# First-layer products in PSUM tiles of their own, the work between products placed piece by piece, twelve plain steps

## The chip, the core and the metric

One core of a Trainium2 chip. Five engines work in parallel, each through its own instructions in order: PE (TensorE, matmuls into PSUM), DVE (VectorE), ACT (ScalarE), POOL (GpSimd) and SP (SyncE, which issues most DMAs). They wait for each other by semaphores. PSUM has eight banks of 128 x 512 f32. The metric is the time of one execution on the device in microseconds (us), the median of several runs.

## The reference

The input x is 2048 x 576 (S x D), f32.

```python
def layernorm(x): return (x - mean(x)) / sqrt(var(x) + 1e-5)      # over D
X = rfft2(layernorm(x)) * (w_r + 1j * w_i)
h = x + irfft2(X)
out = h + relu(layernorm(h) @ w1) @ w2      # w1 576 x 4608, w2 4608 x 576
```

## The kernel before, in words

**First part.** Normalisation, the forward Fourier transform along D and S as matmuls with constant matrices, the product with the filter, and the inverse transform. Its last rows are normalised again and transposed into four chunks `xc[0..3]` of 512 tokens; each chunk holds a high and a low part, since f32 products are made of three matmuls with fp32r operands: high x high, high x low, low x high. `split` (L321) makes such a pair: ACT copies with rounding (the high part), another engine subtracts (the low part, L323).

**The MLP in blocks.** The 4608 hidden units are 18 blocks `g` of 256. *Plain steps*, one per block and chunk, are listed in `steps` (L522): `mm1` (28 matmuls of 512 columns) makes the hidden values, `relu_split` (L560) splits them, `mm2` (48 matmuls of 288 columns) multiplies by w2, and DVE adds the result to `xs` in SBUF (L556). There are eight such steps, (0, 0) to (1, 2). During them `sum_jobs` prepares sums of chunks, stores them to DRAM and `load_sum` (L615) brings them back when wanted.

**Doubles.** From block `FIRST` = 2 on, two chunks are taken together (a *double*: block g, pair p) in 2 x 2 block form with seven products in place of eight, in both layers. `l1_prod(d, r)` (L727) is product r = 0..6 of the first layer of double d, six or eight matmuls of 512 columns, into one of the banks `a` (alternating between doubles), `b`, `c`:

- r = 0, 1, 3, 6 write `a`, each on top of the last: 0 makes A11 B11; once it is copied out (`p1`, L738), 1 adds S2 T2; once that is copied out (`u2`), 3 adds S3 T3; once that is copied out (`c2`), 6 adds A22 T4.
- r = 2 writes `c` (S1 T1); it is added to `c2` after r = 3 (L747); then r = 5 adds S4 B22 to `c`, which is added to `u2` (L756).
- r = 4 writes `b`; it is added to `p1` (L751).

The hidden values are relu of `p1`, `c2`, `u2` and of the final `a` ("late": only finished after r = 6). The second layer takes them, and sums of them, again in split form, for two hidden sets: Z (from `u2` and `c2`: A2, A11, and the sums S12, S34 that four POOL subtractions make in `hsum`, L731 to L734) and Y (from `p1` and the late `a`). `prod` (L789) is one second-layer product, six matmuls of 288 columns, into one of two PSUM tiles `wps[0]`, `wps[1]` in turn, on top of what stands there; `add` (L794) is the DVE addition into `xs`, which must be done before the next product goes into the same tile.

**The order.** It is the order of the Python code, per engine; nothing is rescheduled. `slot(d)` does for r = 0..6: first-layer product r of double d + 1, second-layer products 2r and 2r + 1 of double d with their adds, then `l1_late(d, r)` and `l1_post(d + 1, r)` (the copies, relus, sums and splits), then `weights(d, r)` (splits and sums for the next block: L644 to L648 and `w1_split` for w1, L677 to L680 and `w2_split` for w2; a block lasts two slots, even and odd, `turn` 0 and 1). So products 0 to 6 of the second layer belong to Z, 7 to 13 to Y, and Y's late part is split in the slot in which it is used. `slot_last` ends it with plain second-layer products. The last plain step, step 7, does the first layer of double 0 beside its own four `mm2`.

PSUM: one pool `ps` of four buffers of two banks each. `wps[2]` holds both `a` banks, `wps[3]` holds `b` and `c`. Waits follow tiles: an instruction that writes one half of such a tile also waits for readers of the other half.

Of the kernel before, what the change touches and what calls it, by code (L numbers as in the profile page):

```python
# [128 lines left out]
def kernel(ctx: ExitStack, tc: tile.TileContext, x, w_r, w_i, w1, w2, cc2, c1, fb, ib, c3, out):  # L129
    nc = tc.nc  # L130
    pool = ctx.enter_context(tc.tile_pool(name="sb", bufs=1))
    psum = ctx.enter_context(tc.tile_pool(name="ps", bufs=1, space=PSUM))
# [19 lines left out]
    def act(o, i, **kw):  # L152
        nc.scalar.activation(o, i, AF.Copy, **kw)  # L153
# [368 lines left out]
    steps = [(0, 0), (0, 1), (0, 2), (1, 1), (1, 0), (0, 3), (1, 3), (1, 2)]  # L522
    FIRST = 2
# [94 lines left out]
    wps = [None] * 4  # L618
# [87 lines left out]
    doubles = [(g, p) for g in range(FIRST, NG) for p in ((0, 1) if g % 2 == 0 else (1, 0))]  # L706
# [22 lines left out]
    def hsum(p0, p1, o):  # L729
        s1, s2, s3, s4 = (sums[:, 256 * k:256 * k + 256] for k in range(4))  # L730
        nc.gpsimd.tensor_add(s1, p0[:, 256:], p1[:, 256:])  # L731
        nc.gpsimd.tensor_sub(s2, s1, p0[:, :256])  # L732
        nc.gpsimd.tensor_sub(s3, p0[:, :256], p0[:, 256:])
        nc.gpsimd.tensor_sub(s4, p1[:, :256], s2)  # L734

    def l1_post(d, r):

        a, b, c = (l1_bank(d, n_) for n_ in "abc")  # L738
        p1, u2, c2 = fx["p1"][d % 2], fx["u2"], fx["c2"]
        Z, Y = HF["Z"], HF.get("Y")  # L740
        if r == 0:
            act(p1, a)
        elif r == 1:
            act(u2, a)
        elif r == 3:
            act(c2, a)
            nc.vector.tensor_add(c2, c2, c)  # L747
            relu(c2, c2)
            split(*Z["A2"], c2)
        elif r == 4:  # L750
            nc.vector.tensor_add(p1, p1, b)  # L751
            relu(p1, p1)
            if 0 < d < LAST:
                split(*Y["A11"], p1[:, :256])
        elif r == 5:
            nc.vector.tensor_add(u2, u2, c)  # L756
            relu(u2, u2)
            hsum(u2, c2, None)
            split(*Z["A11"], u2[:, :256])
        elif r == 6:  # L760
            split(*Z["S12"], sums[:, :512])
            split(*Z["S34"], sums[:, 512:])
            if d == LAST:
                split(*Y["S12"], p1)

    def l1_late(d, r):

        a = l1_bank(d, "a")
        p1, c2 = fx["p1"][d % 2], fx["c2"]
        Y = HF["Y"]  # L770
        if r == 0:
            relu_split(Y["A2"], a)
            if d < LAST:
                relu(c2, a)
                hsum(p1, c2, None)
        elif d < LAST:
            if r == 1:
                split(*Y["S12"], sums[:, :512])
            elif r == 2:
                split(*Y["S34"], sums[:, 512:])  # L780

    def prod(z, a, b, bank, first, end=True, whole=True):
        ah, al = a if isinstance(a, tuple) else HF[z][a]
        bh, bl = b if isinstance(b, tuple) else W2[b]
        P = wps[bank].rearrange("p (a n) -> p a n", a=2)[:, :, :288]
        for tt in range(2):
            q = slice(128 * tt, 128 * tt + 128)
            for n_, (l, r) in enumerate(((ah, bh), (ah, bl), (al, bh))):
                nc.tensor.matmul(P[:, tt], l[:, q], r, start=first and n_ == 0, stop=end and n_ == 2, skip_group_check=whole and not first)  # L789

    def add(c, bank, hs, hd):
        P = wps[bank].rearrange("p (a n) -> p a n", a=2)[:, :, :288]
        xt = xs[:, CH * c + 2 * hs:CH * c + 2 * hs + 2, 288 * hd:288 * hd + 288]
        nc.vector.tensor_add(xt, xt, P)  # L794

# [23 lines left out]
    def weights(d, r):  # L819

        g, p = doubles[d]
        if g == NG - 1:
            return
        turn = d % 2
        if turn:
            if r == 0 and g + 2 < NG:
                load_w1(g + 2, vs[1])
            if r == 2:
                w2_sums()
            if r == 4:  # L830
# [98 lines left out]
    for i in range(3, len(steps)):  # L929
        if i == 3:  # L930
            load_weights(FIRST)
            vs[1], vs[2] = raw[FIRST]
        if i == 5:
            vs["s"] = ebuf([128, 1152])
            w2_bufs()
            w2_sums()
        if i == 6:
            w1_bufs()
            w2_split("B22", nc.gpsimd)
            w2_split("T12", nc.gpsimd)  # L940
        if i < 7:
            for q in range(4):
                if q < 2:
                    mm1(i + 1, q)
                mm2(i, q)
                for _ in range(2 if i < 6 else 3):
                    if jobs:
                        jobs.pop(0)()
            continue
        while jobs:  # L950
            jobs.pop(0)()
        w2_split("T34", nc.gpsimd)
        w1_sums()
        for n_ in ("A11", "S12", "S34", "A2", "W4", "wd"):
            w1_split(n_, nc.gpsimd)
        load_w1(FIRST + 1, vs[1])
        FT = sb([128, 4096], "F", dt=F32R)
        TF.update(T1=khalf(3, 0), T2=khalf(1, 0))
        for k, n_ in ((0, "T3"), (1, "T4")):
            TF[n_] = tuple(v2d(FT[:, 2048 * k + 1024 * j:2048 * k + 1024 * j + 1024]) for j in range(2))  # L960
        for n_ in ("T2", "T1", "T3", "T4"):
            load_sum(doubles[0][1], n_)
        fbin = [ebuf([128, 1024]) for _ in range(2)]
        fx.update(p1=(fbin[0][:, :512], fbin[1][:, :512]), u2=fbin[0][:, 512:], c2=fbin[1][:, 512:])
        wps[2:] = [ps(), ps()]
        hidden_bufs("Z")
        for r in range(7):
# [3 lines left out]
            l1_post(0, r)  # L971
# [34 lines left out]
```

## Time and profile before

| | us |
|---|---|
| runs (3) | 1360.06 to 1363.88, median 1361.53 |
| profiled execution | 1363.99 |
| its span, first to last instruction | 1362.2 |
| mean granted PE clock | 0.914 |
| PE busy | 1071.8 (79%) |
| DVE busy | 808.0 (59%) |
| POOL busy | 548.4 (40%) |
| ACT busy | 452.2 (33%) |

In the chain of waits and the timeline a row is: start in us from the span's start, length in us, then engine, line and, in the timeline, operation, written tile <- read tiles, shape and count; in brackets the idle time of the engine before it and what ended that. Matmul lengths overlap, since they are pipelined: the pitch from one start to the next is what they cost when PE is full. The granted clock is a share of full speed. Tiles: `A` holds `xs` and the sums, `d` any PSUM tile, `X`, `B`, `C`, `F` chunks, their sums and second-layer weights, `D` hidden parts, `e` shared buffers (among them `p1`, `u2`, `c2` and the first-layer weights).

### The profile page before, as it was taken

Reading aid. Unit: us, or ns where it says so; the run is one execution under the profiler, and the core shown is the slowest. Engines: PE = TensorE matmul, PEld = TensorE weight load, DVE = VectorE, ACT = ScalarE, POOL = GpSimd, SP = SyncE. Lnnn points to the kernel's source line nnn. Section 1 sums busy time; section 2 is a strip of 40 time slices with the busy share of each in tenths; the row PEclk is TensorE's granted clock in tenths of the full one; section 3 lists DMA queues with packets and bytes.
Section 4 is the critical chain, followed back from the end, with each engine's and each line's share of the span. In section 5 each row is a group of like instructions: output and inputs, shape, how many; then the busy total and the mean of one; then the engine's idle time right before and its main releaser. Section 6 shows DMA issues by size and latency. Waiting matters only on the chain.

```text
span 1362.2 us, 17410 instructions
## 1 busy us (share of the span) xinstructions
PE 1071.8 (79%) x6702; PEld 926.5 (68%) x6702; DVE 808.0 (59%) x1181; ACT 452.2 (33%) x836; POOL 548.4 (40%) x658
## 2 busy tenths in 40 slices
PE   7999999567777777777777777777777777777777
PEld 6776889456666666666666666666666666666666
DVE  7688658525555555555555555555555565555555
ACT  5444442213232333333333333333333333333331
POOL 5005533514343445353435353534444444444421
PEclk8999999789999999999989999988888988888989
DMA  9824113370404040404041313131313222222224
GB/s 247 197 76 103 38 37 124 127 281 4 154 11 152 10 152 20 141 20 141 20 141 29 133 34 127 35 127 52 109 54 107 65 96 79 82 80 81 66 85 113
DMA packets 53987, 127.68 MB, mean 94 GB/s; under 512 B 5392, under 2 KB 25232, under 8 KB 53904
## 3 DMA queue, kind: packets, MB, share of 16 engines
q1 hardware_dynamic: 53168, 125.68, 29.4%
q8 instruction: 53, 0.87, 0.3%
q10 hardware_dynamic: 736, 0.89, 0.2%
q14 instruction: 30, 0.25, 0.1%
HBM read 113.43 MB, written 13.11 MB: 93 GB/s over the span
## 4 chain that ended last, share of the span: by engine, by line
PE 44%; DVE 21%; POOL 7%; ACT 6%; issue 4%; DMA 0%; DVEq 0%; SPq 0%; POOLq 0%
PE d L727 24%; PE d L789 19%; DVE A L794 10%; DVE X L323 5%; ACT e L566 3%; POOL A L732 2%; POOL A L731 2%; POOL A L734 2%; ACT X L153 2%; DVE D L563 1%; DVE e L751 1%; DVE e L747 1%; DVE e L756 1%; ACT e L153 1%; DMA B<-t0T 0%
## 5 line engine op out<-in xcount | busy, mean ns | idle before, releaser
L794 DVE TENSOR_TENSOR A<-A,d 128x576 f32<-128x576 f32 x445 | 332.1, 752 | 331.1 <-PE d L789 319.9
L727 PE MATMUL d<-B,e 128*128 128x512 f32 x528 | 189.5, 498 | 222.5 <-ACT e L153 163.1
L727 PEld LDWEIGHTS d<-B,e 128*128 128x128 f32 x528 | 118.4, 238 | 262.1 <-ACT e L153 170.5
L789 PE MATMUL d<-X,D 128*128 128x288 f32 x1548 | 264.8, 319 | 3.6 <-DVE D L563 2.0
L789 PEld LDWEIGHTS d<-X,D 128*128 128x128 f32 x1548 | 254.9, 214 | 18.0 <-DVE D L563 2.2
L153 ACT ACTIVATE e<-d 128x512 f32<-128x512 f32 (+2 forms) x144 | 85.0, 590 | 290.4 <-PE d L727 245.0
L323 POOL TENSOR_TENSOR X<-e,X 128x576 fp32r<-128x576 f32 (+1 forms) x49 | 74.4, 1532 | 239.1 <-ACT X L153 239.1
L566 ACT ACTIVATE e<-e 128x512 f32<-128x512 f32 x96 | 60.7, 632 | 312.1 <-DVE e L756 123.9
L731 POOL TENSOR_TENSOR A<-e,e 128x256 f32<-128x256 f32 x48 | 35.4, 737 | 264.8 <-ACT e L566 264.8
L323 POOL TENSOR_TENSOR e<-e,e 128x256 fp32r<-128x256 f32 (+2 forms) x65 | 86.7, 1344 | 123.6 <-ACT e L153 123.6
L727 PE MATMUL d<-F,e 128*128 128x512 f32 x384 | 99.4, 394 | 0.0
L727 PE MATMUL d<-X,e 128*128 128x512 f32 x304 | 81.0, 403 | 23.1 <-DVE e L751 23.1
L789 PEld LDWEIGHTS d<-X 128*128 128x128 f32 x576 | 83.1, 188 | 6.0 <-issue 0.8
L789 PE MATMUL d<-X 128*128 128x288 f32 x576 | 86.7, 295 | 0.6 <-DVE A L794 0.6
L789 PE MATMUL d<-X,e 128*128 128x288 f32 x496 | 84.7, 295 | 0.0
L727 PEld LDWEIGHTS d<-X,e 128*128 128x128 f32 x304 | 56.1, 195 | 36.1 <-DVE e L751 26.9
L727 PE MATMUL d<-C,e 128*128 128x512 f32 x224 | 61.1, 400 | 23.1 <-DVE e L747 23.1
L727 PEld LDWEIGHTS d<-F,e 128*128 128x128 f32 x384 | 68.8, 188 | 11.3
L789 PEld LDWEIGHTS d<-X,e 128*128 128x128 f32 x496 | 74.0, 188 | 2.7
L323 DVE TENSOR_TENSOR D<-A,D 128x512 fp32r<-128x512 f32 x63 | 66.8, 1060 | 1.3 <-ACT D L153 1.3
L323 DVE TENSOR_TENSOR X<-e,X 128x256 fp32r<-128x256 f32 (+2 forms) x48 | 41.5, 864 | 37.1 <-ACT X L153 36.7
L727 PEld LDWEIGHTS d<-C,e 128*128 128x128 f32 x224 | 39.9, 188 | 33.9 <-DVE e L747 26.8
(141 smaller groups left out, 1693.6 us busy)
## 6 DMA issues: line engine op xcount, KB each, us to landing
F<-t0T SPq DMA_DIRECT2D x36, 512.0 KB, 4.6
F<-t1T SPq DMA_DIRECT2D x32, 512.0 KB, 4.6
e<-in_B_w_dram SPq DMA_DIRECT2D x18, 576.0 KB, 3.8
e<-in_B_w_dram SPq DMA_DIRECT2D x18, 512.0 KB, 3.7
B<-t0T SPq DMA_DIRECT2D x18, 512.0 KB, 4.6
X<-t0T SPq DMA_DIRECT2D x18, 512.0 KB, 4.8
B<-t1T SPq DMA_DIRECT2D x16, 512.0 KB, 4.5
X<-t1T SPq DMA_DIRECT2D x16, 512.0 KB, 4.8
```

The costliest lines, as they stand in the source:

```text
L153: nc.scalar.activation(o, i, AF.Copy, **kw)
L323: eng.tensor_sub(l, v, h)
L563: nc.vector.scalar_tensor_tensor(l, p, 0.0, h, op0=ALU.max, op1=ALU.subtract)
L566: nc.scalar.activation(o, i, AF.Relu)
L727: nc.tensor.matmul(o, a, b, start=bool(first) and n_ == 0, stop=n_ == len(ops) - 1, skip_group_check=not first)
L731: nc.gpsimd.tensor_add(s1, p0[:, 256:], p1[:, 256:])
L732: nc.gpsimd.tensor_sub(s2, s1, p0[:, :256])
L734: nc.gpsimd.tensor_sub(s4, p1[:, :256], s2)
L747: nc.vector.tensor_add(c2, c2, c)
L751: nc.vector.tensor_add(p1, p1, b)
L789: nc.tensor.matmul(P[:, tt], l[:, q], r, start=first and n_ == 0, stop=end and n_ == 2, skip_group_check=whole and not first)
L794: nc.vector.tensor_add(xt, xt, P)
```

## The change

Five things, all in the MLP.

1. *PSUM.* The pool `ps` is closed in the last plain step, and a second pool opened: four one-bank tiles `h` (`wps[2..5]`: `a` even, `a` odd, `b`, `c`), and two two-bank tiles `w` for second-layer products. Products of `slot_last` that used `wps[2]`, `wps[3]` use pairs of `h` tiles, with an add per tile.
2. *Pieces.* `hsum`, `l1_post` and `l1_late` are replaced by `piece`, one small step per name, and by `PRE` and `PLAN`, which say after which product each stands: `(r, 0)` behind first-layer product r, `(r, 1)` and `(r, 2)` behind the two second-layer products.
3. *Weights.* In odd slots W4 (r = 0), A2 and wd (r = 1) are split, with `load_w1` behind them (r = 1 for r = 0); in even ones T34 and B22 (r = 0, of the block about to be used). Low parts of W4, wd and T34 are on DVE.
4. *Plain steps.* Twelve for eight: block 2 is done in plain steps too, in the order of chunks 3, 1, 0, 2; `FIRST` = 3, so 30 doubles for 32, 29 slots and `slot_last`.
5. *Weights and sums for the first double* are made in steps 8 to 10, the sums loaded in step 10, in place of the last step. One or two sum jobs stand behind each `mm2`, in place of two or three.

```diff
-    steps = [(0, 0), (0, 1), (0, 2), (1, 1), (1, 0), (0, 3), (1, 3), (1, 2)]
-    FIRST = 2
+    steps = [(0, 0), (0, 1), (0, 2), (1, 1), (1, 0), (0, 3), (1, 3), (1, 2), (2, 3), (2, 1), (2, 0), (2, 2)]
+    FIRST = 3
...
     def l1_bank(d, n_):
         k = {"a": d % 2, "b": 2, "c": 3}[n_]
-        return wps[2 + k // 2][:, 512 * (k % 2):512 * (k % 2) + 512]
+        return wps[2 + k]
...
+    PLAN = {
+        (0, 0): "p1c", (0, 1): "", (0, 2): "z3l yAl ys1 ys2 ys3 ys4",
...
+        (6, 2): "z1h z1l",
+    }
+    PRE = "z3h yAh yc2"
...
+        if not turn and r == 0 and d:
+            w2_split("T34", nc.vector)
+            w2_split("B22", nc.gpsimd)
         if g == NG - 1:
             return
-        turn = d % 2
         if turn:
-            if r == 0 and g + 2 < NG:
-                load_w1(g + 2, vs[1])
-            if r == 2:
+            if r == 0:
+                w1_split("W4", nc.vector)
+            if r == 1:
+                w1_split("A2", nc.gpsimd)
+                w1_split("wd", nc.vector)
+                if g + 2 < NG:
+                    load_w1(g + 2, vs[1])
+            if r == 3:
                 w2_sums()
...
-            if r == 6:
-                w2_split("T34", nc.vector)
-                w2_split("B22", nc.gpsimd)
...
-            if r == 3:
+            if r == 4:
                 w1_split("S12", nc.gpsimd)
...
-            if r == 6:
-                for n_ in ("A2", "W4", "wd"):
-                    w1_split(n_, nc.gpsimd)
 
     def slot(d):
+        pieces(d, PRE)
         for r in range(7):
             l1_prod(d + 1, r)
-            for m in (2 * r, 2 * r + 1):
-                second(d, m)
-            l1_late(d, r)
-            l1_post(d + 1, r)
+            pieces(d, PLAN.get((r, 0), ""))
+            second(d, 2 * r)
+            pieces(d, PLAN.get((r, 1), ""))
+            second(d, 2 * r + 1)
+            pieces(d, PLAN.get((r, 2), "").replace("yBh yBl", "" if d == LAST - 1 else "yBh yBl"))
             weights(d, r)
...
+        for q in range(4):
+            if q < 2:
+                mm1(i + 1, q)
+            mm2(i, q)
+            for _ in range(1 + (q == 3)):
+                if jobs:
+                    jobs.pop(0)()
+            if i in (5, 6) and q == 1:
+                split_weights(2, i - 5)
+            if i == 9:
+                (lambda: w2_split("B22", nc.gpsimd), lambda: w2_split("T12", nc.gpsimd), lambda: w2_split("T34", nc.gpsimd), w1_sums)[q]()
+            if i == 10:
+                for n_ in (("A11",), ("S12",), ("S34", "wd"), ("A2", "W4"))[q]:
+                    w1_split(n_, nc.gpsimd)
+    for i in (END,):
...
+        first_banks.close()
+        banks.append(ctx.enter_context(tc.tile_pool(name="pw", bufs=1, space=PSUM)))
+        wps[2:] = [banks[0].tile([128, 512], F32, tag="h", name=f"h_{k}", bufs=4) for k in range(4)]
```

**ACT at the border of two slots.** A slot's last piece on ACT is the high half of Z's S34 sum (`X` <- `A`); then come the late high half of Y (L562, after the change L770), the relu of the late `a` (L566, L572) and the copy of product 0 (L153, L158: `e` <- the other `a`). Before, at the end of an even slot:

```order
L153 ACTIVATE D_2807<-A_1376 128x512
L153 ACTIVATE X_2065<-A_1376 128x512
L153 ACTIVATE e_2660<-e_2335 128x512
L153 ACTIVATE e_2660<-e_2335 128x256
L153 ACTIVATE cc_2661<-e_2549 128x128
L562 ACTIVATE D_2948<-d_2804 128x512
L566 ACTIVATE e_2803<-d_2804 128x512
L153 ACTIVATE e_2802<-d_2804 128x512
```

After:

```order
L158 ACTIVATE D_3183<-A_1376 128x512
L158 ACTIVATE X_2065<-A_1376 128x512
L770 ACTIVATE D_3322<-h_3179 128x512
L572 ACTIVATE e_3173<-h_3179 128x512
L158 ACTIVATE e_3172<-h_3178 128x512
L158 ACTIVATE e_3056<-e_2743 128x256
```

The three weight splits left this place, a smaller one stands behind the copy; the late `a` and the bank of product 0 are now different tiles.

**DVE at the same border.** The low halves of Z's sums (`D`, `X` <- `A`), the adds (L794, after the change L847) and the late low half of Y (L563, L772). Before, at the end of an odd slot:

```order
L323 TENSOR_TENSOR D_2807<-A_1376,D_2807 128x512
L323 TENSOR_TENSOR X_2065<-A_1376,X_2065 128x512
L323 TENSOR_TENSOR X_2065<-e_2549,X_2065 128x576
L794 TENSOR_TENSOR A_1376<-A_1376,d_2945 128x2x288
L794 TENSOR_TENSOR A_1376<-A_1376,d_2946 128x2x288
L563 SCALAR_TENSOR_TENSOR D_2948<-d_2804,D_2948 128x512
```

After:

```order
L747 TENSOR_TENSOR D_3183<-A_1376,D_3183 128x512
L847 TENSOR_TENSOR A_1376<-A_1376,w_3319 128x2x288
L847 TENSOR_TENSOR A_1376<-A_1376,w_3320 128x2x288
L747 TENSOR_TENSOR X_2065<-A_1376,X_2065 128x512
L772 SCALAR_TENSOR_TENSOR D_3322<-h_3178,D_3322 128x512
L328 TENSOR_TENSOR X_2065<-e_2847,X_2065 128x576
```

The S34 low half and T34's (`X` <- `e`) moved behind the first two adds of the new slot, and the late low half is followed, no longer preceded, by T34's.

**PE, first-layer products 3 to 5.** Before (the second-layer rows, L789, between them):

```order
L727 MATMUL d_2804<-F_2793,e_2659 128x512 x6
...
L727 MATMUL d_2805<-B_1393,e_2660 128x512 x7
L727 MATMUL d_2805<-B_1393,G_2662 128x512
L789 MATMUL d_2945<-X_2065,D_2948 128x288 x6
L789 MATMUL d_2946<-X_2065,D_2949 128x288 x6
L727 MATMUL d_2805<-B_1393,e_2659 128x512 x6
L727 MATMUL d_2805<-B_1393,cc_2661 128x512 x2
```

After:

```order
L733 MATMUL h_3179<-F_3059,e_3055 128x512 x6
...
L733 MATMUL h_3180<-C_1394,e_3056 128x512 x7
L733 MATMUL h_3180<-C_1394,G_3058 128x512
L837 MATMUL w_3319<-X_2065,D_3322 128x288 x6
L837 MATMUL w_3320<-X_2065,D_3323 128x288 x6
L733 MATMUL h_3181<-X_2065,e_3055 128x512 x6
L733 MATMUL h_3181<-X_2065,cc_3057 128x512 x2
```

The order is the same; products 4 (`b`) and 5 (`c`) went into one tile, `d_2805`, and now go into two, `h_3180` and `h_3181`.

More of the change, by code (lines that the diff above doesn't have):

```diff
@@ L142, in ps @@
         n[0] += 1
+        if banks:
+            return banks[0].tile([128, 1024], F32, tag="w", name=f"w_{n[0]}", bufs=2)
         return psum.tile([128, 1024], F32, tag="d", name=f"d_{n[0]}", bufs=4)
+    banks = []
     def ebuf(shape, dt=F32):
@@ L752, in l1_post @@
             relu(p1, p1)
-            if 0 < d < LAST:
-                split(*Y["A11"], p1[:, :256])
-        elif r == 5:
+        elif n_ == "yBh":
+            act(Y["A11"][0], p1[:, :256])
+        elif n_ == "yBl":
+            low(Y["A11"], p1[:, :256])
+        elif n_ == "u2a":
             nc.vector.tensor_add(u2, u2, c)
+        elif n_ == "u2r":
             relu(u2, u2)
[L758 to L780, printed above, removed]
+        elif n_ == "zBh":
+            act(Z["A11"][0], u2[:, :256])
+        elif n_ == "zBl":
+            low(Z["A11"], u2[:, :256])
+        else:
+            raise ValueError(n_)
@@ L782, in prod, with pieces, halves @@
+    PLAN = {
[7 rows of a table added]
+    }
+    PRE = "z3h yAh yc2"
+    def pieces(d, names, first=False):
+        for n_ in names.split():
+            if first and (n_[0] == "y" or n_ == "z3l"):
+                continue
+            piece(d, n_)
+    def halves(bank):
+        if bank < 2:
+            return [wps[bank][:, 512 * k:512 * k + 288] for k in range(2)]
+        return [wps[8 - 2 * bank + k][:, :288] for k in range(2)]
     def prod(z, a, b, bank, first, end=True, whole=True):
@@ L784, in prod @@
         bh, bl = b if isinstance(b, tuple) else W2[b]
-        P = wps[bank].rearrange("p (a n) -> p a n", a=2)[:, :, :288]
+        P = halves(bank)
         for tt in range(2):
@@ L788, in prod @@
             for n_, (l, r) in enumerate(((ah, bh), (ah, bl), (al, bh))):
-                nc.tensor.matmul(P[:, tt], l[:, q], r, start=first and n_ == 0, stop=end and n_ == 2, skip_group_check=whole and not first)
+                nc.tensor.matmul(P[tt], l[:, q], r, start=first and n_ == 0, stop=end and n_ == 2, skip_group_check=whole and not first)
     def add(c, bank, hs, hd):
+        if bank >= 2:
+            for k, P in enumerate(halves(bank)):
+                xt = xs[:, CH * c + 2 * hs + k, 288 * hd:288 * hd + 288]
+                nc.vector.tensor_add(xt, xt, P)
+            return
         P = wps[bank].rearrange("p (a n) -> p a n", a=2)[:, :, :288]
@@ L936 @@
             w2_sums()
-        if i == 6:
+        if i == 10:
+            while jobs:
+                jobs.pop(0)()
             w1_bufs()
[L939 to L955, printed above, removed]
-        load_w1(FIRST + 1, vs[1])
[L957 to L962, printed above, removed]
+            FT = sb([128, 4096], "F", dt=F32R)
@@ L970 @@
                 mm2(i, r // 2)
-            l1_post(0, r)
+            for k in range(3):
+                pieces(-1, PLAN.get((r, k), ""), first=True)
             if r == 0:
```

87 lines of the change are left out of this document (66 added, 21 removed), and 5 rows, old and new, of the table PLAN.

## The prediction

> **What bounds the kernel now.** I read the page's busy line first, then the chain of waits in one slot, then the timeline of the same slot, then stretches of the span. No engine is full:
>
> ```profile
> PE 1071.8 (79%) x6702; PEld 926.5 (68%) x6702; DVE 808.0 (59%) x1181; ACT 452.2 (33%) x836; POOL 548.4 (40%) x658
> ```
>
> So it is a chain. Slots (one double each, `slot`) fill 301.12 to 1341.29 us: the first row below is `l1_prod(1, 0)`, where slot 0 begins, the second is product 0 of `slot_last`.
>
> ```profile
> 301.12 1.54 PE L727 MATMUL d<-C,e 128*128 128x512 f32 x6
> ...
> 1341.29 1.02 PE L789 MATMUL d<-X 128*128 128x288 f32 x6 [0.59 <-DVE A L794]
> ```
>
> 1040.17 us over 31 slots is 33.55 us each. The chain of waits across one slot border (start, length, what):
>
> ```profile
> 700.20 0.61 DVE e L756
> ...
> 700.83 0.64 ACT e L566
> ...
> 701.54 0.75 POOL A L731
> ...
> 704.59 0.64 ACT X L153
> ...
> 705.25 2.94 DVE X L323 x2
> 708.20 0.67 DVE A L794
> ...
> 708.96 0.75 DVE A L794
> 709.72 0.61 DVE D L563
> ...
> 710.35 0.60 ACT e L566
> 710.95 0.50 ACT e L153
> ...
> 711.49 2.93 PE d L727 x6
> ...
> 716.36 1.85 PE d L727 x8
> 718.21 1.59 PE d L789 x12
> 719.80 1.39 PE d L727 x6
> ```
>
> It starts when first-layer product 5 is in PSUM: add (L756), relu, four sums on POOL (L731 to L734), the high half (ACT), two low halves on DVE, two adds, the late low half (L563), relu, and the copy of product 0 out of PSUM (L153). Only then may product 1 overwrite that bank: 11.3 us from 700.20 to 711.49. The timeline of the slot shows PE paying for it:
>
> ```profile
> 711.49 2.93 PE L727 MATMUL d<-B,e 128*128 128x512 f32 x6 [5.75 <-ACT e L153]
> 714.21 2.15 PE L789 MATMUL d<-X,D 128*128 128x288 f32 x12
> ...
> 724.22 1.89 PE L727 MATMUL d<-C,e 128*128 128x512 f32 x7 [1.44 <-DVE e L747]
> ...
> 729.39 1.66 PE L727 MATMUL d<-X,e 128*128 128x512 f32 x6 [1.44 <-DVE e L751]
> ...
> 743.84 2.93 PE L727 MATMUL d<-B,e 128*128 128x512 f32 x6 [4.37 <-ACT e L153]
> ```
>
> Three idle stretches per slot: 4.37 or 5.75 us before product 1, 1.44 us each before products 4 and 5. After the long one six matmuls take 2.93 us where six take 1.39 us later (719.80): the granted clock is half. The stretches (busy us of PE, PEld, DVE, ACT, POOL, then the granted clock, DMA share and GB/s):
>
> ```profile
> 240.00:252.80 12.80, 12.79 (x77) 11.42 (x75) 7.79 (x8) 2.68 (x4) 6.29 (x3) 1.00 0.32 129
> 252.80:284.00 31.20, 8.58 (x22) 5.99 (x23) 7.94 (x8) 7.25 (x13) 11.88 (x13) 0.58 0.53 194
> ...
> 711.49:743.84 32.35, 25.10 (x134) 21.93 (x134) 18.94 (x25) 10.93 (x21) 15.96 (x20) 0.92 0.03 8
> 743.84:778.60 34.76, 26.10 (x135) 22.92 (x136) 19.79 (x26) 10.60 (x19) 13.50 (x16) 0.89 0.46 151
> ...
> 717.00:743.80 26.80, 19.59 (x114) 17.12 (x112) 17.58 (x24) 8.87 (x17) 12.11 (x14) 0.97 0.04 9
> ```
>
> **The floor of a slot.** Products 0, 1 and 3 have six matmuls, 1.39 us; products 2, 4, 5 and 6 have eight, 1.85 us; seven pairs of second-layer products 1.60 us each (three rows from 716.36 on). 3 x 1.39 + 4 x 1.85 + 7 x 1.60 = 22.77 us. The two slots above check it: 67.11 us, less idle 15.9 (7.25 and 8.66: length minus PE busy), is 51.2; less 2 x 22.77 leaves 5.7 us, the half clock. So 10.8 us of the mean slot are waits and their consequences.
>
> **The change, part by part.**
>
> Durations come from the groups by line and form over all slots; between the bars stand busy us and the mean ns of one:
>
> ```profile
> L794 DVE TENSOR_TENSOR A<-A,d 128x576 f32<-128x576 f32 x274 | 204.5, 752 | 205.1 <-PE d L789 198.3
> ...
> L789 PE MATMUL d<-X 128*128 128x288 f32 x354 | 53.3, 295 | 0.6 <-DVE A L794 0.6
> ...
> L323 POOL TENSOR_TENSOR e<-e,e 128x512 fp32r<-128x512 f32 x27 | 42.2, 1578 | 58.9 <-ACT e L153 58.9
> ...
> L323 DVE TENSOR_TENSOR X<-A,X 128x512 fp32r<-128x512 f32 x19 | 29.6, 1557 | 2.9 <-ACT X L153 1.5
> ...
> L323 DVE TENSOR_TENSOR e<-A,e 128x512 fp32r<-128x512 f32 x19 | 13.0, 685 | 0.0
> ...
> L323 DVE TENSOR_TENSOR X<-e,X 128x576 fp32r<-128x576 f32 x9 | 12.1, 1340 | 0.0
> L323 DVE TENSOR_TENSOR X<-e,X 128x256 fp32r<-128x256 f32 x19 | 11.8, 622 | 21.8 <-ACT X L153 21.8
> ...
> L323 POOL TENSOR_TENSOR X<-e,X 128x288 fp32r<-128x288 f32 x9 | 11.1, 1236 | 0.0
> ...
> L562 ACT ACTIVATE D<-d 128x512 fp32r<-128x512 f32 x19 | 10.9, 575 | 0.0
> ```
>
> *Own PSUM tiles.* Before, the two `a` banks are halves of one tile and `b` and `c` of another. Product 4 writes `b` but waits for L747, which reads `c`; product 5 writes `c` and waits for L751, which reads `b`. After, each has its tile; product 5's true condition, the read of `c` after product 3, lies one product earlier and ahead of that step's adds. 2 x 1.44 us per slot go, and nothing takes their place: `c2a` ends about 12.3 us into the slot (product 3 ends at 10.8; copy 0.6, add 0.68, handovers), product 5 begins at 15.9.
>
> *The order of pieces at the border.* ACT now runs the late high half, the relu and the copy right behind the S3/S4 high half; the DVE low halves come behind them. From the chain 705.25 to 710.33, 5.1 us, leaves; the late high half, 0.57 us (L562), comes in. What is left, from product 5's end: 0.2 (the last matmul lasts 295 ns where the pitch is 1.60 / 12 = 0.133, and a handover) + 0.61 + 0.66 + 3.0 (four sums, 701.54 to 704.59) + 0.64 + 0.57 + 0.60 + 0.50, with some 0.3 of handovers: 7.1 us. PE has, between the end of product 5 and the start of the next product 1, 1.60 + 1.85 + 1.60 + 1.39 + 1.60 = 8.04 us of work. The wait is covered with 0.9 us to spare, and with it goes the half clock. If POOL is late with the sums by more than that, the excess comes back as a wait.
>
> *DVE order.* A second-layer product may run 2.2 us or more (0.8 for its neighbour, 1.39 to 1.85 first layer) after its bank's last use, and an add needs 0.2 + 0.76, so adds may come about 1.3 us late before PE notices. Work on DVE per slot: 14 adds x 0.75 = 10.5; nine 512-wide pieces x 0.68 = 6.1; two 256-wide 1.1 (0.62 or less each); weights 0.7 (W4, wd) or 1.34 (T34, at the border of even slots): 18.4 to 19.0 of 22.77 us. The same low half costs 0.685 us in one place and 1.557 us in the other, where it meets POOL splits (1.578 us each):
>
> ```profile
> 738.26 3.42 POOL L323 TENSOR_TENSOR e<-e,e 128x512 fp32r<-128x512 f32 x2
> ...
> 739.00 1.54 DVE L323 TENSOR_TENSOR X<-A,X 128x512 fp32r<-128x512 f32 x1 [0.15 <-ACT X L153]
> ```
>
> Five such pieces at the long price are 4.4 us more, 22.8 to 23.4 in all. Walked through step by step, the worst place is the even slot: T34's low half ends 6.6 us into it, the next two adds 8.1, and product pair 2 needs them at 8.6; the following pieces leave the copy some 0.2 us late. I take 0.6 us of stall per slot: 23.4, near the floor, because the border has 0.9 us and the adds 1.3 us of slack. Ends: 22.77 (no stall) and 25.0 (DVE full at 23.4 plus 1.6, a POOL split queued ahead of the sums once).
>
> [...]
>
> *Weight preparation over both slots.* A2, W4 and wd move to odd slots, T34 and B22 to the start of even ones. POOL's share was 15.96 and 13.50 us of work per slot; 23.4 us still hold it. First uses: B22's low half follows Y's four sums on POOL, of which the third waits for a DVE low half until 4.6 us into the slot, so 6.2 + 1.24 = 7.5 against 8.6 (the tightest); A2's ends near 8.1 against 12.4. ACT's high half behind those sums ends by 7.4; the copy of product 3 queued behind it can run only from 11.0. `load_w1` moves behind A2's split on SP, and the four sum loads behind it wait up to 8 us; they are needed a slot later. I cost this at nothing; PE and the 0.9 us above cover it, and if B22 came 1 us later than I have it, the cost is 0.5 us every other slot.
>
> *Twelve plain steps.* Four more steps, two doubles fewer. A plain step lasts 12.76 us, PE full:
>
> ```profile
> 214.35 3.36 PE L150 MATMUL d<-X,e 128*128 128x512 f32 x14
> ...
> 227.11 3.36 PE L150 MATMUL d<-X 128*128 128x512 f32 x14
> ```
>
> 4 x 12.76 = 51.0 us, ending at 252.8 + 51.0 = 303.8. Sum jobs, splits and loads of the last step now lie under these (DVE was busy 7.8 of 12.8 us, DMA 0.32). Behind 252.80 the trace has 48.3 us until 301.12, for a last step with 50 x 0.231 + 4 x 1.60 = 18.0 us of work, while PE waits at a clock of 0.58. Now the inputs are there; I add 1.0 for emptying the old PSUM pool and 0.9 for the copy before product 1 (no second-layer work covers it there): 19.9. Ends: 18 and 25.
>
> *The end* keeps its 20.9 us (1341.29 to 1362.2); Y's first split, moved here, stands on ACT and DVE where PE waited 1.99 us before; ends 19 and 23.
>
> **Sum.** 252.8 + 51.0 + 19.9 + 29 x 23.4 (678.6) + 20.9 = 1023.2 us, plus 1.8 us that the profiled execution (1363.99) has beyond its span (1362.2): 1025 us. That execution lies 0.2% above the median of the runs, 1361.53.
>
> **Rivals.**
> - *DVE becomes the bound.* For it: 18.9 and 19.8 us busy already, less room, more POOL beside it. Against it: adds, over half of DVE, stay at 0.752 us whatever POOL does. Slot 25 to 26: 1025 + 29 x 1.6 to 2.6 = 1071 to 1100 us.
> - *The border chain still reaches product 1,* by a POOL split ahead of the sums: 1.58 - 0.9 = 0.7 us, with 0.6 more on alternate slots; slot 24.4, 1054 us. Against it: the split's high half comes from ACT 2 us before the sums.
> - *Slower.* The many short waits could hold the clock at half throughout: 22.77 x 2 = 45.5 us a slot, 344.6 + 29 x 45.5 + 1.8 = 1666 us; it decides for slower once more than half of the matmuls run so (slot above 35.1 us). Against it: the 1.44 us gaps left the clock at 0.97 in 717.00:743.80; only 4.4 us and more halved it. [...]
> - *The plain part does not pack:* waits on weights or buffers in the four added steps and the last one as in 252.80:284.00 (22 us idle): 1047 us.
>
> **Chances.** Forecast (slot 22.8 to 24) 0.58; DVE 0.2; border chain 0.1; plain part 0.07; slower 0.04; 0.01 no change. Range: 1003 (all lower ends) to 1095 (slot near 25.8). Less than 0.3% either way (4 us) cannot be told from no change; faster 0.95.
>
> **What would show it.** Slots of 23 to 24 us; no ACT wait above 1 us before product 1 and none from L782 or L790 before products 4 and 5; clock near 1.00 in all slots; DVE at 80 to 90% of a slot; about 20 us, not 48, between the last full plain step and slot 0. I am wrong if adds are what PE waits for in most steps, or if product 1 still waits for ACT.

## The result, and the profile after

The changed kernel takes 1003.12 us (median of four runs, 1003.00 to 1003.34), beside 1361.77 us for the kernel before on the same chip: a ratio of 0.7366, 95% interval 0.7353 to 0.7379. The prediction was 1025 us with a range of 1003 to 1095; the result lies at its lower edge. The profiled execution took 1003.0 us, its span is 1001.2 us. One execution of one variant below (only `b` and `c` shared) took 1379.08 us at a mean granted clock of 0.654, where its other three took 1008.6 to 1010.6 us, and is left out of that variant's number.

The busy line and the chain of waits of the changed kernel's page:

```profile
PE 980.7 (98%) x6738; PEld 870.0 (87%) x6738; DVE 773.1 (77%) x1182; ACT 436.5 (44%) x802; POOL 516.1 (52%) x596
...
PE 93%; DVE 4%; DMA 1%; ACT 1%; issue 0%; POOL 0%; ACTq 0%; DVEq 0%
```

PE is busy 98% of the span where it was 79%, and the chain is PE for 93%: it is no longer a chain through other engines. PE's timeline from the last full plain step to the end:

```profile
299.17 4.95 PE L155 MATMUL d<-e,D 128*128 128x288 f32 x36
...
305.05 1.61 PE L733 MATMUL h<-B,e 128*128 128x512 f32 x6 [0.94 <-DVE A L562]
...
307.39 1.67 PE L733 MATMUL h<-B,e 128*128 128x512 f32 x6 [0.74 <-ACT e L158]
...
324.01 1.54 PE L733 MATMUL h<-C,e 128*128 128x512 f32 x6
...
982.46 1.03 PE L837 MATMUL w<-X 128*128 128x288 f32 x6
...
985.57 0.79 PE L837 MATMUL h<-X,D 128*128 128x288 f32 x4 [1.02 <-DVE D L328]
```

The plain steps end near 303.9 us, slot 0 begins at 324.01, `slot_last` at 982.46. The last plain step takes 20.1 us (48.3 before), the 29 slots 658.45 us, 22.71 each (33.55 before, and 22.77 was the floor from the rows of before), the end 18.7 us (20.9 before). The stretches (busy us of PE, PEld, DVE, ACT, POOL, then granted clock, DMA share, GB/s):

```profile
252.80:303.80 51.00, 51.00 (x306) 46.47 (x305) 31.08 (x33) 12.08 (x17) 18.94 (x17) 1.00 0.50 183
303.80:324.01 20.21, 18.54 (x101) 15.87 (x100) 6.12 (x9) 5.32 (x9) 4.62 (x6) 1.00 0.67 215
...
500.00:600.00 100.00, 100.00 (x593) 90.64 (x593) 81.54 (x116) 48.77 (x91) 65.30 (x72) 1.00 0.39 135
982.46:1001.20 18.74, 12.64 (x90) 12.03 (x90) 11.22 (x18) 1.43 (x4) 1.00 (x1) 0.93 0.59 158
```

In the slots PE has no idle time, but for 0.8 us in the first one, and the clock is 1.00; before it was 0.89 to 0.92. One slot border, PE and ACT of the timeline:

```profile
574.40 1.53 PE L733 MATMUL h<-B,e 128*128 128x512 f32 x6
...
577.36 1.54 PE L733 MATMUL h<-B,e 128*128 128x512 f32 x6
```

```profile
574.70 0.58 ACT L770 ACTIVATE D<-h 128x512 fp32r<-128x512 f32 x1
575.18 0.59 ACT L572 ACTIVATE e<-h 128x512 f32<-128x512 f32 x1
575.97 0.60 ACT L158 ACTIVATE e<-h 128x512 f32<-128x512 f32 x1 [0.20 <-PE h L733]
```

The copy of product 0 (575.97) now waits for PE, 0.20 us, where PE waited 4.4 or 5.8 us for that copy. It ends 0.8 us before product 1 starts (577.36). So about 1.0 us is to spare at the border.

### The profile page after: what moved, and what is told of

It is laid out like the page before. It is cut to its first block, busy times and chain, and to the rows that moved or that the text cites. A ratio compares the mean times of both kernels' runs of the same rounds, so it can differ in the third digit from the quotient of the medians.

```text
span 1001.2 us, 17471 instructions
## 1 busy us (share of the span) xinstructions
PE 980.7 (98%) x6738; PEld 870.0 (87%) x6738; DVE 773.1 (77%) x1182; ACT 436.5 (44%) x802; POOL 516.1 (52%) x596
## 4 chain that ended last, share of the span: by engine, by line
PE 93%; DVE 4%; DMA 1%; ACT 1%; issue 0%; POOL 0%; ACTq 0%; DVEq 0%
PE h L733 34%; PE w L837 33%; PE d L155 24%; DMA X<-in_A_x_dram 1%; DVE st L215 1%; PE d L513 1%; PE w L155 0%; DVE A L473 0%; PE h L837 0%; DVE e L492 0%; DVE D L569 0%; DVE e L491 0%; DVE e L374 0%; DVE A L562 0%; DVE mv L216 0%
## 5 line engine op out<-in xcount | busy, mean ns | idle before, releaser
L847 DVE TENSOR_TENSOR A<-A,w 128x576 f32<-128x576 f32 x415 | 307.0, 751 | 80.7 <-PE w L837 65.0
L837 PE MATMUL w<-X,D 128*128 128x288 f32 x1428 | 219.0, 295 | 0.8 <-DVE A L562 0.8
L837 PEld LDWEIGHTS w<-X,D 128*128 128x128 f32 x1428 | 206.0, 188 | 10.9 <-DVE A L562 1.0
L733 PE MATMUL h<-B,e 128*128 128x512 f32 x495 | 131.0, 393 | 1.7 <-DVE A L562 0.9
L158 ACT ACTIVATE e<-h 128x512 f32<-128x512 f32 x90 | 54.0, 600 | 179.7 <-PE h L733 179.7
L328 POOL TENSOR_TENSOR e<-e,e 128x512 fp32r<-128x512 f32 (+2 forms) x61 | 78.3, 1284 | 71.9 <-ACT e L158 71.9
L572 ACT ACTIVATE e<-e 128x512 f32<-128x512 f32 x90 | 56.9, 633 | 122.7 <-DVE e L798 55.0
L733 PEld LDWEIGHTS h<-B,e 128*128 128x128 f32 x495 | 88.9, 188 | 17.0 <-ACT e L158 1.2
L733 PE MATMUL h<-F,e 128*128 128x512 f32 x360 | 93.1, 394 | 0.0
L837 PEld LDWEIGHTS w<-X 128*128 128x128 f32 x540 | 77.7, 188 | 5.1 <-issue 0.3
L837 PE MATMUL w<-X 128*128 128x288 f32 x540 | 81.0, 295 | 0.1
L837 PE MATMUL w<-X,e 128*128 128x288 f32 x464 | 79.3, 295 | 0.0
L158 ACT ACTIVATE e<-e 128x256 fp32r<-128x256 f32 (+3 forms) x110 | 57.1, 533 | 1.6 <-POOL e L381 0.7
```

Of the source, the lines that this page charges most:

```text
L328: eng.tensor_sub(l, v, h)
L572: nc.scalar.activation(o, i, AF.Relu)
L733: nc.tensor.matmul(o, a, b, start=bool(first) and n_ == 0, stop=n_ == len(ops) - 1, skip_group_check=not first)
L837: nc.tensor.matmul(P[tt], l[:, q], r, start=first and n_ == 0, stop=end and n_ == 2, skip_group_check=whole and not first)
```

## The experiments

### Each part alone, on the kernel before

**Own PSUM tiles alone**: the second pool, a tile for each bank, nothing else.

```diff
-        return wps[2 + k // 2][:, 512 * (k % 2):512 * (k % 2) + 512]
+        return wps[2 + k]
...
-        wps[2:] = [ps(), ps()]
+        first_banks.close()
+        banks.append(ctx.enter_context(tc.tile_pool(name="pw", bufs=1, space=PSUM)))
+        wps[2:] = [banks[0].tile([128, 512], F32, tag="h", name=f"h_{k}", bufs=4) for k in range(4)]
```

> The kernel before with only the PSUM part of the change: own one-bank tiles for a even, a odd, b, c and two tiles for second-layer products; order of pieces, weights and eight plain steps as before. Theory (the waits before products 4 and 5 are false ones, from shared tiles, and the border wait before product 1 is the chain's): the two waits of 1.44 us go, the 4.4 to 5.8 us before product 1 and the half clock behind it stay; 31 x 2.9 = 90 us less, about 1272 us. Rival (the chain at the border sets the slot's length whatever lies before it, so time saved at products 4 and 5 is waited at product 1): within 15 us of before.

Measured: 1269.9 us, ratio 0.932 (0.929 to 0.935), 92 us less. PE's timeline of this kernel, its only rows with a wait in two slots:

```profile
643.30 2.92 PE L732 MATMUL h<-B,e 128*128 128x512 f32 x6 [4.88 <-ACT e L158]
...
674.93 2.93 PE L732 MATMUL h<-B,e 128*128 128x512 f32 x6 [6.30 <-ACT e L158]
```

The waits before products 4 and 5 are gone, 92 / 31 = 3.0 us a slot; the wait at the border and its half clock (2.93 us for six matmuls) stay.

**The new order of pieces alone**, with the old halves of tiles.

```diff
+        pieces(d, PRE)
         for r in range(7):
             l1_prod(d + 1, r)
-            for m in (2 * r, 2 * r + 1):
-                second(d, m)
-            l1_late(d, r)
-            l1_post(d + 1, r)
+            pieces(d, PLAN.get((r, 0), ""))
+            second(d, 2 * r)
...
```

> The kernel before with only the new order of pieces; PSUM tiles shared, weights and plain steps as before. Theory: products 4 and 5 no longer wait even with shared tiles, since the reads of c and b now stand ahead of the adds; but product 1 waits for the late low half, which reads the other half of its tile and stands on DVE behind two adds and a low half, until about 5.3 us into the slot against 3.0: 2.3 us, too short for the half clock. Slot 25.1 us: 301 + 31 x 25.1 + 21 + 2 = 1102 us. Rival (own tiles are needed for products 4 and 5 too): 2.9 us more, slot 28, about 1190 us.

Measured: 1222.5 us, ratio 0.897 (0.893 to 0.902). Both numbers missed. PE's timeline, again all rows with a wait in some 60 us:

```profile
595.59 2.79 PE L727 MATMUL d<-B,e 128*128 128x512 f32 x6 [2.59 <-ACT e L566]
...
602.50 2.87 PE L727 MATMUL d<-B,e 128*128 128x512 f32 x6 [2.12 <-DVE D L766]
...
625.47 1.65 PE L727 MATMUL d<-B,e 128*128 128x512 f32 x6 [1.26 <-ACT e L566]
...
630.82 1.66 PE L727 MATMUL d<-B,e 128*128 128x512 f32 x6 [2.12 <-DVE D L766]
```

Products 4 and 5 do not wait, though they share a tile: their readers now stand right behind products 3 and 4. The theory had this right, and the wait before product 1 (2.12 us, 2.3 expected). It missed the wait before product 0, and the half clock behind waits of 2.59 and 2.12 us (six matmuls in 2.79 and 2.87 us; behind the 2.12 us at 630.82 six took 1.66 us). That 2.3 us are too short for the half clock was an estimate that no run had shown. So new waits stand before products 0 and 1. The code says why. `pieces(d, PRE)` reads the late `a` and is now written ahead of product 0, which writes the other half of the same tile; so product 0 waits for the relu (L566), and product 1 for the late low half (L766). In the old order `l1_late` came behind product 0, and no such wait arose.

**The two together**, with the old plain steps and old weight places. The edit is the sum of the two diffs above.

> The kernel before with the own PSUM tiles and the new order of pieces together; eight plain steps and the old places of the weight preparation stay. Each of the two alone took 92 and 139 us. Theory (they are one thing: the order frees products 4 and 5, and only own tiles free products 0 and 1 once the order is new): a slot of 22.71 us as in the changed kernel plus 0.2 to 0.5 us where the old weight splits stand in the way; 301.1 + 31 x 22.71 to 23.2 + 18.7 + 1.8 = 1026 to 1041 us, near 1033. Rival (the two add up): 1361.5 - 92 - 139 = 1131 us.

Measured: 1029.1 us, ratio 0.7555 (0.754 to 0.757), inside the theory's range. The parts gave 92 and 139 us alone, together 333: some 101 us belong to neither alone.

### Parts undone, on the changed kernel

**The old order, with own tiles, twelve steps and spread weights**: the diff of the order, reversed.

```diff
-            pieces(d, PLAN.get((r, 0), ""))
...
+            l1_late(d, r)
+            l1_post(d + 1, r)
```

> The changed kernel with the order of pieces of before put back (copies, relus, sums and splits grouped behind both second-layer products, the late part behind products 0 and 1); own tiles, spread weights, twelve plain steps stay. Theory: the border wait and the half clock come back, products 4 and 5 stay free: slot about 30.5 us, 304 + 20 + 29 x 30.5 + 19 + 2 = 1230 us. Rival (own tiles and spread weights are what freed product 1): below 1060 us.

Measured: 1234.0 us, ratio 0.906 (0.903 to 0.909), near the theory's 1230. The wait before product 1 and its half clock are back in full:

```profile
638.08 2.93 PE L733 MATMUL h<-B,e 128*128 128x512 f32 x6 [5.00 <-ACT e L158]
```

**Shared tiles in the new order**: `a` and `a`, `b` and `c` are halves of one tile again.

```diff
-        return wps[2 + k]
+        return wps[2 + k // 2][:, 512 * (k % 2):512 * (k % 2) + 512]
...
-        wps[2:] = [banks[0].tile([128, 512], F32, tag="h", name=f"h_{k}", bufs=4) for k in range(4)]
+        wps[2:] = [banks[0].tile([128, 1024], F32, tag="h", name=f"h_{k}", bufs=2) for k in range(2)]
```

> The changed kernel with the two a banks as halves of one tile again, and b and c of another; all else stays. Theory: only product 1 waits, for the late low half on DVE, 2.3 us in odd and even slots (in even ones T34's split stands behind it): slot 25.0 us, 1003 + 29 x 2.3 = 1070 us. Rival (products 4 and 5 wait again, 2.9 us a slot more): 1150 us. Second rival (the order alone is enough): 1003 us.

Measured: 1142.9 us, ratio 0.839 (0.836 to 0.841), 140 us more than the changed kernel. The theory missed the wait before product 0 and the half clock; the first rival's number is near, but not its reason. PE's waits between 345 and 950 us (total us, times, longest), all there are:

```profile
PE h L733 <- DVE D L772: 47.0, 22, 2.5
PE h L733 <- ACT e L572: 27.8, 22, 1.3
```

These are the waits before products 1 and 0, 3.4 us a slot; none stands before products 4 and 5. After some of the 2.12 us waits the clock is halved as well (below); waits and half clock make nearly all of the 140 / 29 = 4.8 us a slot.

**Only `b` and `c` shared**: the `a` banks keep their own tiles.

```diff
-        wps[2:] = [banks[0].tile([128, 512], F32, tag="h", name=f"h_{k}", bufs=4) for k in range(4)]
+        wps[2:4] = [banks[0].tile([128, 512], F32, tag="h", name=f"h_{k}", bufs=2) for k in range(2)]
+        bc = banks[0].tile([128, 1024], F32, tag="bc", name="bc_0", bufs=1)
+        wps[4:] = [bc[:, :512], bc[:, 512:]]
```

> The changed kernel with b and c as halves of one PSUM tile again, while the two a banks keep their own. Theory (in the new order products 4 and 5 find L782 and L790 done anyway, since the pieces stand right behind products 3 and 4; own tiles pay only at products 0 and 1): 1003 us within 0.3%, with no wait before products 4 and 5; all of the 140 us by which the kernel with both pairs shared is slower belongs to the a pair. Rival (the prediction's first part as written: b and c in one tile cost 1.44 us each before products 4 and 5): 1003 + 29 x 2.9 = 1087 us.

Measured: 1008.6 to 1010.6 us in three executions, ratio 0.7408 (0.7393 to 0.7422). That is 6 us over the changed kernel: neither the theory's nothing nor the rival's 84. The waits are in the last plain step, which has no second-layer work between most products; in a slot only product 4 is a little longer. PE's timeline of this kernel:

```profile
315.37 1.89 PE L733 MATMUL bc<-B,e 128*128 128x512 f32 x7 [1.44 <-DVE e L782]
...
318.27 1.66 PE L733 MATMUL bc<-B,e 128*128 128x512 f32 x6 [0.78 <-DVE e L790]
...
325.23 1.54 PE L733 MATMUL h<-C,e 128*128 128x512 f32 x6
...
338.82 1.88 PE L733 MATMUL bc<-C,e 128*128 128x512 f32 x7
...
987.95 1.03 PE L837 MATMUL w<-X 128*128 128x288 f32 x6
```

In the last step 1.44 and 0.78 us are lost. The 29 slots last (987.95 - 325.23) / 29 = 22.85 us, 0.15 more than in the changed kernel: L782 ends at about the time when product 4 wants to start. So of the 140 us that shared tiles cost in the new order some 134 belong to the `a` pair: this is the difference of the two kernels, as none with the `a` pair alone shared was run.

**The old places of the weight preparation:**

```diff
-        if not turn and r == 0 and d:
-            w2_split("T34", nc.vector)
-            w2_split("B22", nc.gpsimd)
...
+            if r == 6:
+                w2_split("T34", nc.vector)
+                w2_split("B22", nc.gpsimd)
...
+            if r == 6:
+                for n_ in ("A2", "W4", "wd"):
+                    w1_split(n_, nc.gpsimd)
```

> The changed kernel with the weight splits at their old places (A2, W4 and wd at the end of even slots, T34 and B22 at the end of odd ones). Theory (the prediction's border chain with about 1.0 us to spare): ACT's high halves of the three splits, about 1.2 us, and their low halves on POOL come ahead of the border chain; 0.2 to 1.0 us of wait at each second border: 1006 to 1018 us. Rival (PE is covered anyway, the spreading is worth nothing): 1003 us, within 0.2%. Second rival (POOL is late with the four sums by whole splits of 1.58 us, and the half clock returns): above 1040 us.

Measured: 1007.7 us (1007.1 to 1007.9), ratio 0.7397 (0.7386 to 0.7408): 4.5 us more, inside the theory's range. One product in every second slot is late, product 1. PE's timeline, two such places two slots apart:

```profile
372.40 1.66 PE L733 MATMUL h<-B,e 128*128 128x512 f32 x6
...
418.12 1.66 PE L733 MATMUL h<-B,e 128*128 128x512 f32 x6
```

45.72 us lie between them, 2 x 22.71 = 45.42 in the changed kernel. What is ahead of it on ACT, from its timeline:

```profile
369.36 1.02 ACT L158 ACTIVATE X<-e 128x576 fp32r<-128x576 f32 x2 [1.38 <-PE w L837]
```

These are the high halves of T34 and B22 at the end of an odd slot, and right behind them come Z's last high half and the border chain. They run for 1.02 us, which uses up what the border has to spare; 0.3 us in two slots (45.72 against 45.42) is left over as a wait. At the other border, behind A2, W4 and wd, PE has no wait.

**Eight plain steps**, with own tiles, new order and spread weights:

```diff
-    steps = [(0, 0), (0, 1), (0, 2), (1, 1), (1, 0), (0, 3), (1, 3), (1, 2), (2, 3), (2, 1), (2, 0), (2, 2)]
-    FIRST = 3
+    steps = [(0, 0), (0, 1), (0, 2), (1, 1), (1, 0), (0, 3), (1, 3), (1, 2)]
+    FIRST = 2
```

> The changed kernel with the eight plain steps, FIRST = 2 and the old preparation of the first double's inputs: own tiles, new order and spread weights stay. Theory: slots as in the changed kernel (22.71 us), the 48.3 us between the last full plain step and slot 0 come back: 301.1 + 31 x 22.71 + 18.7 + 1.8 = 1025.6 us, so the twelve steps are worth 22 us, of which 28 come from the packed last step and 6 are lost, because two doubles (45.4 us) are cheaper than four plain steps (51.0). Rival (the stall of the last step shrinks by itself once products 0 and 1 have tiles of their own): below 1010 us.

Measured: 1021.5 us, ratio 0.7503 (0.749 to 0.7515). PE's timeline of the last step:

```profile
261.16 1.19 PE L732 MATMUL h<-B,e 128*128 128x512 f32 x2 [9.92 <-DVE A L561]
265.62 2.08 PE L732 MATMUL h<-B,e 128*128 128x512 f32 x4 [3.28 <-POOL e L328]
276.99 0.77 PE L732 MATMUL h<-B,e 128*128 128x512 f32 x1 [9.29 <-DMA B<-t0T]
...
296.17 1.54 PE L732 MATMUL h<-C,e 128*128 128x512 f32 x6
```

PE waits 22.5 us for sums, splits and loads, as it did before the change. The twelve steps are worth 18.3 us here, a little less than the 22 of the theory, which let slot 0 begin at 301.1 us; it begins at 296.17.

**Twelve plain steps alone, on the kernel before:** the four added steps and the earlier preparation.

```diff
-    FIRST = 2
+    FIRST = 3
...
+            if i == 9:
+                (lambda: w2_split("B22", nc.gpsimd), lambda: w2_split("T12", nc.gpsimd), lambda: w2_split("T34", nc.gpsimd), w1_sums)[q]()
+            if i == 10:
+                for n_ in (("A11",), ("S12",), ("S34", "wd"), ("A2", "W4"))[q]:
+                    w1_split(n_, nc.gpsimd)
```

> The kernel before with the twelve plain steps and the early preparation alone; old tiles, old order, old slots. Theory: two slots of 33.55 us go, four plain steps of 12.76 us come, and the last step takes 20.1 us in place of 48.3: 1361.5 - 67.1 + 51.0 - 28.2 = 1317 us. Rival (with the old tiles the last step waits as before): 1345 us.

Measured: 1320.0 us, ratio 0.969 (0.967 to 0.971). The theory's 1317 holds; the slots keep the waits of before. Two of them, from the timeline:

```profile
600.26 2.93 PE L729 MATMUL d<-B,e 128*128 128x512 f32 x6 [5.74 <-ACT e L153]
...
618.95 1.66 PE L729 MATMUL d<-X,e 128*128 128x512 f32 x6 [1.44 <-DVE e L753]
```

### How much is to spare

**The border chain made longer**, by repeating the last of Z's four sums on POOL once, and three times:

```diff
-                nc.gpsimd.tensor_sub(s4, p1_[:, :256], s2)
+                for _ in range(1 + 1 if n_[0] == "z" else 1):
+                    nc.gpsimd.tensor_sub(s4, p1_[:, :256], s2)
```

> The changed kernel with the last of Z's four sums on POOL done twice in each slot (the same result): the border chain is 0.73 us longer. Theory (the border has 0.2 us of idle time on ACT before the copy of product 0 and 0.8 us between the end of that copy and product 1, 1.0 us in all): hidden, 1003 us within 0.3%. Rival (nothing to spare at the border, PE runs without a gap by luck of equal rates): 0.73 us in each of 29 slots, 1024 us.

Measured: 1003.7 us (1003.1 to 1006.5), hidden as the theory has it.

> The changed kernel with the last of Z's four sums on POOL done four times in each slot: the border chain is 2.2 us longer. Theory (1.0 us to spare): 1.2 us of wait before product 1 in 29 slots, without half clock, since the 1.44 us waits of the kernel before left the clock near 1.00: 1003 + 29 x 1.2 = 1038 us, between 1032 and 1045. Rival (another, later condition holds product 1, the sums have room): 1003 us. Second rival (B22's low half, pushed back on POOL too, becomes the next wait, or the half clock comes): above 1055 us.

Measured: 1061.0 us (1059.9 to 1062.0), above the theory's range. The second rival's number is met (above 1055), but not its reason: B22 is not waited for, and the half clock comes in one slot only, the first. PE's waits for the copy in this kernel (total us, times, longest), and three of its product 1:

```profile
PE h L733 <- ACT e L158: 47.8, 30, 2.8
```

```profile
331.04 2.93 PE L733 MATMUL h<-B,e 128*128 128x512 f32 x6 [2.79 <-ACT e L158]
...
578.55 1.66 PE L733 MATMUL h<-B,e 128*128 128x512 f32 x6 [1.58 <-ACT e L158]
...
603.05 1.65 PE L733 MATMUL h<-B,e 128*128 128x512 f32 x6 [1.58 <-ACT e L158]
```

It is the wait the theory named, before product 1, for the copy; a slot lasts 603.05 - 578.55 = 24.50 us, 1.79 more. The delay was larger than set. The chain of waits of this kernel, from product 5's add to the copy, and the same add of the changed kernel:

```profile
618.04 0.70 DVE e L799
...
623.43 0.07 issue
623.50 0.75 POOL A L759
...
624.31 1.07 POOL A L759
...
627.01 0.49 ACT e L158
```

```profile
569.57 0.69 DVE L798 TENSOR_TENSOR e<-e,h 128x512 f32<-128x512 f32 x1 [0.73 <-PE h L733]
```

From the add to the copy 8.97 us now pass. In the changed kernel the relu ahead of the copy lets it go about 0.5 us after 575.18, 6.1 us from the add. So the delay is 2.8 to 2.9 us (each repetition costs a handover of 0.07 us, and the last lasts 1.07 instead of 0.73 us), and 2.8 - 1.79 = 1.0 us were to spare, the theory's number. Of the rest, 4.8 us are in the first slot, whose wait is 2.79 us with the half clock behind it, and 1.8 us in `slot_last`, which has a wait of 2.1 us in place of 1.0.

**More work on DVE**: five of the low halves are made twice.

```diff
-            (eng or nc.vector).tensor_sub(f[1], v, f[0])
+            for _ in range(2 if n_ in 'z1l z3l y1l y3l zAl'.split() else 1):
+                (eng or nc.vector).tensor_sub(f[1], v, f[0])
```

> The changed kernel with five low halves on DVE done twice in each slot (both of Z's and both of Y's sums, and Z's A2): about 4.0 us more DVE work, from 18.9 to 22.9 us of a slot of 22.7. Theory (DVE has slack and its adds may be late; it bites only as it becomes full): slots of 22.9 to 23.7 us, 1009 to 1032 us. Rival (DVE is on the path already; its pieces are waited for): the whole 4.0 us in each slot, 1003 + 29 x 4.0 = 1119 us. Second rival (no effect, as DVE's waits for PE of 58 us take it all): 1003 us.

Measured: 1032.7 us (1032.5 to 1033.2), just above the upper end of the theory. The stretch, the waits of PE for adds, and one of them:

```profile
600.00:700.00 100.00, 97.82 (x568) 86.32 (x567) 92.92 (x135) 45.88 (x86) 61.61 (x67) 1.00 0.37 126
```

```profile
PE w L838 <- DVE A L848: 14.4, 14, 1.2
```

```profile
642.39 1.07 PE L838 MATMUL w<-X,D 128*128 128x288 f32 x6 [1.00 <-DVE A L848]
```

DVE goes from 18.9 us of a slot to 0.929 x 23.65 = 22.0, 3.1 us more, and 0.94 us of them appear: 1.0 us in every second slot, where adds come behind a double low half and the split of wd, the rest in small pieces. The 29 slots give 27 of the 30 us; `slot_last` is 3.4 us longer, with a wait of 3.06 us and the half clock behind it. So the changed kernel has over 2 us of DVE time left in a slot.

## Why the prediction was right, and where it was not

**The total.** 1003.12 us lies inside the range by 0.1 us, and that is in part luck: the slot (22.71 us) and the end (18.7 us) both came out below their lower ends (22.77 and 19), 2.0 us together, and only the last plain step, 2.1 us above its lower end of 18, made up for it. Of the signs that were named, the slots of 23 to 24 us did not come. The others did: a clock near 1.00, DVE at 80 to 90% of a slot (81.5 to 83.3%), some 20 us before slot 0, and no wait before products 1, 4 and 5.

**What bounds the kernel, and the floor.** Right. 22.77 us from three rows of the slow kernel was the length of a slot of the fast one to 0.3% (22.71).

**Own PSUM tiles.** "2 x 1.44 us per slot go" is right for the old order (92 us in 31 slots). Where I placed their worth in the changed kernel was wrong: there the order alone frees products 4 and 5, but for 0.15 us a slot. What the own tiles do in the new order is to keep products 0 and 1 from waiting for the readers of the late `a`; I named the two `a` halves and gave them no price. They are worth about 134 us there. The sum does not show it, as both parts are in the change.

**The order at the border.** Right in size: 0.9 us to spare was predicted, about 1.0 us is there by the trace, by the one repetition that vanished, and by the three that cost 1.79 of 2.8 us. But "with it goes the half clock" holds only with the own `a` tiles; the order alone left 1.3 to 2.6 us before product 0 and 2.1 us before product 1, and the half clock behind the 2.6 us and half of the 2.1 us. "Only 4.4 us and more halved it" was a misreading of the trace of before: there a wait of 2.56 us, at 308.73, is followed by six matmuls in 2.79 us, and one of 1.99 us by a half clock too (1345.10, below).

**DVE order.** This step failed in its size. The 0.6 us of stall per slot are zero; with the 0.09 us by which the floor (22.77 for 22.71) and the rounding to 23.4 were too long, the predicted slot was 0.69 us too long, and 29 x 0.69 = 20 us of the error of 22 us are that. DVE's load without the long prices was right (18.4 to 19.0 predicted, 18.5 to 18.9 measured); the 4.4 us for five pieces at the long price did not come. The stall came from adding prices of before one behind the other at the worst place. The low halves of the changed kernel by form (busy us, mean ns):

```profile
L747 DVE TENSOR_TENSOR D<-A,D 128x512 fp32r<-128x512 f32 x59 | 50.0, 847 | 1.3 <-ACT D L158 1.3
...
L747 DVE TENSOR_TENSOR e<-A,e 128x512 fp32r<-128x512 f32 x29 | 25.2, 870 | 0.0
...
L747 DVE TENSOR_TENSOR X<-A,X 128x512 fp32r<-128x512 f32 x30 | 20.6, 688 | 0.0
L847 DVE TENSOR_TENSOR A<-A,w 128x576 f32<-128x576 f32 x415 | 307.0, 751 | 80.7 <-PE w L837 65.0
```

The one that cost 1.557 us costs 0.688. Before, by the timelines of DVE and POOL, 30 of its 32 overlapped a POOL split and took 1.53 to 1.68 us, and the two that did not (303.69 and 1343.15) took 0.69 us; now one of the 30 overlaps a split, for 0.35 us, and one a sum. The first two forms pay, on average, 0.16 to 0.18 us more than 0.688, and a 256-wide one (`X` <- `e`) 0.93 us where it took 0.62. The longest 512-wide low half of a slot takes 1.24 us, so none pays the long price, and DVE waits 65.0 us for PE before its adds. The run with 3.1 us more work shows that the adds have room.

**Weight preparation.** "I cost this at nothing" holds, with B22's tight 1.1 us included. The old places would have cost 4.5 us, by ACT's high halves ahead of the last part of the border chain.

**Twelve plain steps.** Right: 51.0 us with PE full for 51.00 of 51.00, the last step 20.1 against 19.9, with the two expected waits of 0.94 and 0.74 us. Alone they bring 42 us on the kernel before and 18 on the rest of the change, mainly since the two slots that they replace are worth 33.55 us each there and 22.7 here.

**The end** was predicted unchanged at 20.9 and took 18.7. I had kept a stretch that contained a wait of 1.99 us and a half clock behind it; now the wait is 1.02 us (985.57, above), and the granted clock behind it is 1.00 (985.50 to 990.00), where it was 0.66 (1345.10 to 1350.10). That is the other 2.2 us of the error. The row of before, 24 matmuls in 4.95 us where 24 at the pitch of 0.133 us take 3.2:

```profile
1345.10 4.95 PE L789 MATMUL d<-X,D 128*128 128x288 f32 x24 [1.99 <-DVE D L563]
```

**The rivals.** DVE as the bound: not seen, and it would need more than 2 us more work a slot. The border chain reaching product 1: not seen, 1.0 us away. Half clock throughout: not seen, and no run shows it from short waits (behind 1.26 to 1.58 us the clock was full in all 100 records, below). A plain part that does not pack: not seen in the changed kernel.

## What to carry to other kernels

Dependencies that follow whole tiles depend on where in the program the readers stand. Splitting a tile may be worth little in one order and a great deal in the next (here `b` and `c`: 0.15 us a slot in the new order, 3.0 us in the old), so two such changes should be costed together. In the slots here the waits went, DVE was the busiest of the other engines with 81.5 to 83.3%, and the sum of PE's own work forecast the length to 0.3% (22.77 us for 22.71); a stall is to be charged only where a chain reaches PE with the neighbours that its instructions have after the change, not with those of before. A stretch that is carried over unchanged should first be rid of waits and half clock that the change removes elsewhere.

## What the runs showed of the hardware

In these traces the clock's answer to a wait of PE changes between 1.58 and 2.59 us. I took the six matmuls of 512 columns behind each wait in the slots after the first, in the kernel before and in five of the experiments (own tiles alone, new order alone, old order, shared tiles, the sum done four times). Behind waits of 1.26 to 1.58 us (100 records) six always took 1.63 to 1.66 us. Behind waits of 2.59 us and more (102) they never ran at full speed (2.16 to 2.93 us). Behind waits of 2.05 to 2.12 us (56) it was one or the other, 28 times each; one wait of 2.47 us left the clock full. What decides there is open. With the new order alone, 13 of the 15 waits that followed a half-clock stretch by some 7 us halved the clock again, but only 4 of the 14 that followed a short wait at full clock; in the shared-tile kernel, where all follow a short wait, 11 of 27 did. In the shared-tile kernel the same wait stands one slot apart with both:

```profile
608.83 1.65 PE L733 MATMUL h<-B,e 128*128 128x512 f32 x6 [2.12 <-DVE D L772]
...
635.54 2.93 PE L733 MATMUL h<-B,e 128*128 128x512 f32 x6 [2.12 <-DVE D L772]
```

By these records a wait that is cut from 4.4 us to 1.5 us gives back the 2.9 us by which it is shorter and at least the 1.3 us by which the next six matmuls were slow (2.93 against 1.66 us).
